# Retention and an expert layer in one kernel: keys and values of two batches loaded as one chunk, two tokens per partition, with attention products on quarters of the array

## The chip, the cores and the metric

The kernel runs on one core of a Trainium2 chip. A core has five engines that run their own instruction streams and wait for each other by semaphores: TensorE (PE in the profile; PEld is its loading of weights), VectorE (DVE), ScalarE (ACT), GpSimd (POOL) and SyncE (SP, which here issues DMAs). Data come from HBM by DMA into SBUF (128 partitions); TensorE writes its products into PSUM, and DVE and ACT read them there. POOL reads and writes SBUF alone. The metric is the device time of one execution in microseconds. Before the change it is 218.52 us, the median of three runs (218.41 to 218.56).

## What is computed

Eight batches of eight heads, 576 tokens, 64 numbers per head. The attention has no softmax: scores are multiplied with a decay that depends on the distance of the tokens. Its output, 4608 tokens of 512, goes through a layer with a softmax-weighted activation and a normalisation.

```python
def _attn_ref(q, k, v) -> np.ndarray:
...
    scores = scale * np.matmul(q, k.transpose(0, 1, 3, 2))
    gamma = 1.0 - 2.0 ** (-5.0 - np.arange(H, dtype=np.float32))
...
    Dmat = np.where(rel >= 0, gamma[:, None, None] ** rel[None, :, :], 0.0)
    ret = scores * Dmat[None, :, :, :]
    return np.matmul(ret, v).astype(np.float32)
...
def _moe_ref(x, w_in, w_out, g_ln) -> np.ndarray:
    h = x @ w_in
    h_max = np.max(h, axis=-1, keepdims=True)
    e = np.exp(h - h_max)
    sm = e / (np.sum(e, axis=-1, keepdims=True) + 1e-09)
    solu = h * sm
    mu = np.mean(solu, axis=-1, keepdims=True)
    var = np.mean((solu - mu) ** 2, axis=-1, keepdims=True)
    ln = (solu - mu) / np.sqrt(var + 1e-06) * g_ln
    return (ln @ w_out).astype(np.float32)
```

Inputs and output are float32; w_in is 512x1024, w_out 1024x512.

## The kernel before

**Chunks.** The 4608 tokens are cut into 36 chunks of 128. For every two batches there are nine: four chunks of 128 tokens of each batch, in turns (chunk 0 is batch 0 tokens 0 to 127, chunk 1 the same of batch 1), and one mixed chunk with the last 64 tokens of both. Token p of a chunk has partition p.

**Decay.** gamma to the power i-j is split into gamma^i on the queries and gamma^-j on the values, both counted from the chunk's first token. So scores need only a triangular mask of ones. What earlier chunks contribute goes through a running state (64x64 per head): per chunk the product of keys and values is added to the decayed state of before.

**Steps of one chunk n**, each a small function that issues a few instructions (lines are those of kernel.py):

- `ld` (L178): three DMAs from SP for queries, keys and values, 256 KB each. A key or value packet is 256 bytes (64 numbers of one token and head). Queries are read in another arrangement, with packets of 1 KB. The mixed chunk has two DMAs of each kind.
- `cq`, `ck`, `cv` (L205, L218, L223): scaling or casting to float16. The letter behind the chunk in the written order names the engine: a ACT, v DVE, g POOL.
- `tq` with `eq`, `tr` with `er`, `kd`, `kq` (L226 to L281): the transposes. PE turns 128x128 blocks into PSUM and DVE or ACT copies them out; `kd` instead lets a DMA turn the keys, from chunk 12 on.
- `sc` (L283): scores. For four pairs of heads, two products with 64 rows each, on the upper and lower half of the array, into two PSUM banks. `mk` (L296): DVE multiplies each of the two with the mask (128x512).
- `kv` (L306): keys times values, eight products with 64 columns. `ad` (L320): DVE adds the decayed state and gives `t`. `d3` (L347): POOL multiplies `t` with gamma^128 for the next chunk's addition; `dk` (L334): POOL makes the float16 state for PE.
- `av` (L358): masked scores times values, eight products with 64 output partitions each, one bank. `fs` (L372): queries times state, added in the same bank. `ex` (L388): copied out as `xT`.
- `m1` (L406; `mr` L393 for the first two, by rows of w_in): xT times w_in, eight matmuls of 512 columns, into one of two PSUM tiles `h`. `mx` (L418): DVE takes the negated row maximum. `xp` (L425): ACT makes exp and its sum. `so` (L433): DVE multiplies h and exp into `u` and sums it; after it the `h` tile is free.
- `ce` (L445): for chunks below 5 the mean is taken off `u`. From 5 on it is in the centred weights `w_c`, made by `mm`, `mc`, `ws` after `wo` has scaled w_out. `wi` casts w_in.
- `sq` (L458): ACT sums squares. `rt` (L471): three small POOL instructions give the reciprocal root. `tu` and `eu` (or `du` by DMA): transposes of `u`. `m2` (L508): times w_out, eight matmuls of 512 columns. `st` (L520): ACT scales, SP stores.
- The last chunk's layer is done in halves by `hm` to `hw`.

**Order.** There is no scheduler: the three texts START, LOOP and END write out in which order the steps are issued, as step:chunk:engine. START holds the first steps up to the point where LOOP takes over, LOOP is repeated for 21 chunks, END drains. Every engine takes its own instructions in that order, SP its DMA issues too.

**Buffers.** PSUM has eight banks: four for `h` and four that BANKS hands out, one digit per request. SBUF tiles come from rotating pools (six or seven loads, five queries, four `xT` and so on); a step waits until the last user of its buffer is done.

Of the kernel before, what the change touches and what calls it, by code (L numbers as in the profile page):

```python
# [10 lines left out]
FP = mybir.dt.float32  # L11
# [3 lines left out]
H = 8  # L15
# [3 lines left out]


PLAIN = 5
FIRST = 7
STEP = 1
STOP = 28
BY_DMA = 12
START = """
ld:0 ld:1 c1:0 ck:0:g cq:0:v cv:0:v li:3 gt:0 c2:0 tq:0 cq:1:g cv:1:v ld:2 kv:0 ck:1:v tq:1 ad:0
eq:1:a d3:0 cq:2:v cv:2:g li:2 li:0 eq:0:a kv:1 wi:3:1:a sc:1 li:1 mk:1 dk:0 sc:0 ck:2:a ld:4
av:1 wi:3:0:a wi:2:1:g fs:1 tq:2 ld:3 mk:0 ad:1 av:0 ex:1:a wi:0:0:g eq:2:a fs:0 wi:1:1:a kv:2
mr:1:3 ad:2 d3:1 wi:1:0:g wi:2:0:v cq:4:g wi:0:1:v d3:2 sc:2 mr:1:0 ex:0:v ld:5 mr:1:2 ld:6  # L30
mr:1:1 mr:0:0 mr:0:2 mk:2 ck:4:g mx:1 xp:1 mr:0:1 mr:0:3 av:2 dk:1 mx:0 tq:4 eq:4:a so:1 cv:4:g
ce:1 wu:0:4 fs:2 lo:1 lo:2 cq:3:v sc:4 ex:2:a ck:3:g cv:3:g tu:1 xp:0 mk:4 m1:2 sq:1 tq:3 eu:1:a
dk:2 kv:4 eq:3:a ck:5:a kv:3 av:4 cq:5:g so:0 fs:4 ad:3 d3:3 sc:3 mx:2 dk:3 cq:6:g ex:4:a mk:3
ad:4 tq:5 cv:5:g xp:2 eq:5:a m1:4 lo:0 lo:3 sc:5 d3:4 so:2 cv:6:g mk:5 dk:4 kv:5 av:3 ck:6:a
fs:3 tq:6 d3:6 wo:4:g av:5 ex:3:a ld:7 eq:6:a wo:1:g mx:4 ad:5 wo:7:g kv:6 xp:4 m1:3 fs:5 ce:0
ce:2 wo:2:a ex:5:a tu:0 tu:2 sc:6 wo:5:a m1:5 ld:8 ad:6 so:4 wo:3:a eu:2:v mk:6 rt:1 wo:6:v
wo:0:a sq:0 d3:5 av:6 sq:2 mx:5 fs:6 ck:7:g mm:0 m2:1 cq:7:g ld:9 mx:3 eu:0:a rt:2 mc:0:v m2:0
ce:4 cq:8:v ws:3:v rt:0 xp:3 tu:4 ex:6:a ws:7:v ld:10 ws:4:v ck:8:g dk:5 st:1 xp:5 tq:7 sq:4
so:3 eu:4:v ld:11 eq:7:a m2:2 st:0 so:5 tq:8 ce:3 eq:8:a m1:6 ws:1:v ws:0:v cv:7:g sc:7 ws:2:g
tu:3 st:2 rt:4 ws:5:v ld:12 m2:4 mk:7 sc:8 sq:3 eu:3:a cq:9:g mx:6 mk:8 m2:3 st:4 dk:6 rt:3  # L40
cq:10:g kv:7 ck:9:a ws:6:v xp:6 cv:9:v ad:7 cv:8:v st:3 av:7 fs:7 ex:7:a ck:10:a ck:11:a
"""
LOOP = """
tr:2 so:-1 tu:-2 ld:6 er:2:v m1:0 dk:0 kv:1 eu:-2:a kd:4 ad:1 cv:3:g av:1 mx:0 sc:2 sq:-2 fs:1
ex:1:a rt:-2 cq:4:g xp:0 m2:-2 d3:0 ck:5:g st:-2 mk:2
"""
END = """
d3:-7 tr:-5 kd:-3 cq:-3:g kv:-6 av:-6 er:-5:v ld:-1 ad:-6 tr:-4 fs:-6 ex:-6:a dk:-7 sq:-9
so:-8 sc:-5 m1:-7 cv:-4:g er:-4:v mk:-5 tr:-3 kd:0 kv:-5 ck:-2:g av:-5 sq:-8 fs:-5 tu:-8 mx:-7
ad:-5 rt:-9 cv:-3:g dk:-5 er:-3:a tu:-9 kd:-2 m1:-6 xp:-7 sc:-4 kv:-4 cq:-2:v eu:-9:v so:-7  # L50
ex:-5:a m1:-5 sc:-3 mk:-4 rt:-8 du:-7 d3:-6 ld:0 mx:-6 eu:-8:a d3:-5 mk:-3 ad:-4 ck:-1:a dk:-6
m2:-9 av:-4 mx:-5 xp:-6 kv:-3 av:-3 d3:-4 cv:-1:g st:-9 d3:-1 ad:-3 kd:-1 cv:-2:g d3:-2 cq:0:g
fs:-4 fs:-3 so:-6 tr:-2 er:-2:v ex:-4:a xp:-5 m2:-8 sq:-6 dk:-4 sc:-2 mk:-2 ck:0:g m1:-4 so:-5
kv:-2 kv:-1 du:-5 ex:-3:a av:-2 sq:-7 st:-8 mx:-4 sq:-5 xp:-4 fs:-2 m1:-3 cq:-1:v cv:0:g kq:-1
rt:-5 dk:-3 ex:-2:a d3:-3 ad:-2 du:-6 tr:0 so:-4 er:0:a m2:-7 sc:0 m1:-2 ad:-1 mk:0 mx:-3
sc:-1 rt:-6 mk:-1 mx:-2 m2:-5 sq:-4 du:-4 kv:0 rt:-7 rt:-4 av:-1 av:0 fs:-1 dk:-1 m2:-6 st:-7
xp:-3 so:-3 ex:-1:v xp:-2 so:-2 du:-3 du:-2 dk:-2 sq:-3 st:-6 fs:0 m1:-1 rt:-3 ex:0:a st:-5
sq:-2 hm:0:0 hm:0:1 m2:-3 mx:-1 hx:0:0 hx:0:1 xp:-1 hp:0:1 so:-1 m2:-2 hp:0:0 ho:0:1 ho:0:0
du:-1 ht:0:1 hc:0 st:-3 ht:0:0 m2:-4 he:0:1:v sq:-1 hq:0:0:v he:0:0:v rt:-2 rt:-1 ad:0
hq:0:1:a h2:0:0 rt:0 m2:-1 h2:0:1 st:-4 st:-2 hw:0:0:a st:-1 hw:0:1:v  # L60
# [3 lines left out]
012312012012302130312031321320132103123120132130123012301230123012301230213021320132012301230213  # L64
021320132012301230213021320132013201321032103120312013201321032103120312013201321032103120312031
203102310210321032120312310213230213210213023201203203
# [3 lines left out]
def _np_tables():  # L70


    g = 1.0 - 2.0 ** (-5.0 - np.arange(H, dtype=np.float64))
    p = np.arange(P)
    gq = (g[None, :] ** p[:, None]) / 8.0
    gk = g[None, :] ** (-p[:, None])
    j = np.arange(8)
    gqt = (g[2 * (p[:, None] % 4) + j // 4] ** (4 * (p[:, None] // 4) + j % 4)) / 8.0
    gqm = (g[2 * (p[:, None] % 4) + j // 4] ** ((4 * (p[:, None] // 4) + j % 4) % 64)) / 8.0
    gkt = g[None, :] ** (-(p % 64)[:, None])  # L80


    gs = np.zeros((P, 4))
    gd = np.zeros((P, 4, 2))
    for e in range(2):
        for hp in range(4):
            gs[e * 64 : e * 64 + 64, hp] = g[2 * hp + e] ** 128.0
        gd[e * 64 : e * 64 + 64, :, e] = gs[e * 64 : e * 64 + 64]
    small = np.concatenate([gq, gk, gqt, gkt, gs, gd.reshape(P, 8), gqm], axis=1).astype(np.float32)
    return small  # L90
# [3 lines left out]
def kernel(  # L94
# [79 lines left out]
    def quads(n):  # L174

        return n != NCH - 2
# [28 lines left out]
    def cq(n, e="g"):  # L205
        if not quads(n):
            return scaled(n, "qf", "q16", gq, ENG[e])
# [570 lines left out]
```

## Time and profile before

| what | value |
|---|---|
| median of three runs | 218.52 us |
| the profiled execution | 218.18 us, span 216.5 us |
| PE busy | 197.4 us (91%), 1989 matmuls |
| DVE busy | 180.8 us (84%) |
| POOL busy | 173.6 us (80%) |
| ACT busy | 167.1 us (77%) |
| packets of the main DMA queue | 111904, 46.55 MB, 92.7% of 16 engines' span |

The span runs from the first to the last instruction of the profiled execution; the time of that execution is 1.7 us longer. PE's busy time counts a matmul until its modelled end, and matmuls overlap: the 264 of L412 have a mean of 379 ns each but start 216 ns apart. So what an instruction costs an engine is read from the distance of starts, and the work that PE has to do is less than its busy time.

### The profile page before, as it was taken

The numbers are of one execution on the slowest core, as the hardware profiler recorded it, in microseconds if no ns is written. First come the engines' busy times: TensorE is split into PE (matmuls) and PEld (weight loads), VectorE is DVE, ScalarE is ACT, GpSimd is POOL, SyncE is SP. The second block draws the span as 40 slices with busy tenths as digits, with TensorE's granted clock in tenths as the row PEclk, the third lists the DMA queues.
The fourth block names the chain that finished last, engine by engine and source line by source line (L and its number), as shares of the span: only waits on it lengthen the run. The fifth ranks groups of instructions, "written<-read, shape, count | busy, mean of one in ns | idle before, by whom it ended". The sixth has DMA issues, their size and how long they took to land.

```text
span 216.5 us, 5376 instructions
## 1 busy us (share of the span) xinstructions
PE 197.4 (91%) x1989; PEld 110.8 (51%) x1989; DVE 180.8 (84%) x289; ACT 167.1 (77%) x279; POOL 173.6 (80%) x275
## 2 busy tenths in 40 slices
PE   0379889896999999999999999999999999999993
PEld 0254456453455555555555555555555565545451
DVE  1378899999997998888888898888888999889840
ACT  2073988966897888888888788888888794986991
POOL 3348889997367899999997899999997899977340
PEclk9999999999999999999999999999999999999999
DMA  5999999998986899799999998899999999674845
GB/s 137 289 317 287 228 280 358 193 245 224 270 228 168 219 183 201 177 225 258 243 223 232 255 208 186 186 247 248 214 227 213 253 181 190 145 172 100 195 109 182
DMA packets 112250, 47.04 MB, mean 217 GB/s; under 512 B 96984, under 2 KB 106208, under 8 KB 112224
## 3 DMA queue, kind: packets, MB, share of 16 engines
q1 hardware_dynamic: 111904, 46.55, 92.7%
q8 instruction: 15, 0.25, 0.5%
q10 hardware_dynamic: 320, 0.16, 0.3%
q14 instruction: 11, 0.09, 0.2%
HBM read 32.54 MB, written 9.44 MB: 194 GB/s over the span
## 4 chain that ended last, share of the span: by engine, by line
PE 78%; DVE 13%; DMA 2%; issue 2%; SPq 2%; ACT 1%; DVEq 0%; ACTq 0%
PE o L515 26%; PE h L412 23%; PE sc L290 5%; PE lp L495 5%; PE x L365 4%; PE x L380 3%; PE kp L314 3%; DVE nm L422 3%; DVE ret L303 2%; DMA vf<-in_v_dram 2%; PE tp L232 2%; PE tr L256 2%; PE h L400 2%; DVE u L437 2%; DVE q L210 1%
## 5 line engine op out<-in xcount | busy, mean ns | idle before, releaser
L412 PE MATMUL h<-w_in,xT 128*128 128x512 f16 x264 | 62.4, 379 | 0.5 <-DVE u L437 0.5
L515 PE MATMUL o<-w_c,uT 128*128 128x512 f16 x240 | 56.5, 379 | 0.6 <-DVE t L327 0.4
L428 ACT ACTIVATE e<-h,nm 128x1024 f32<-128x1024 f32 x35 | 39.0, 1116 | 14.0 <-DVE nm L422 14.0
L303 DVE TENSOR_TENSOR ret<-sc,tris 128x512 f16<-128x512 f32 x72 | 46.1, 682 | 1.3 <-PE sc L290 1.2
L437 DVE SCALAR_TENSOR_TENSOR u<-h,e 128x1024 f16<-128x1024 f32 x35 | 42.7, 1220 | 2.7 <-ACT e L428 1.4
L422 DVE TENSOR_REDUCE nm<-h 128x1 f32<-128x1024 f32 x35 | 42.5, 1216 | 2.0 <-PE h L412 1.5
L515 PEld LDWEIGHTS <-uT 128*128 128x128 f16 x280 | 26.2, 98 | 27.1 <-issue 0.4
L412 PEld LDWEIGHTS <-xT 128*128 128x128 f16 x264 | 24.2, 98 | 24.4 <-issue 0.5
L341 POOL TENSOR_TENSOR s<-t,small 128x512 f16<-128x512 f32 x32 | 34.2, 1070 | 2.6 <-DVE t L329 2.6
L199 POOL TENSOR_TENSOR v<-vf,small 128x512 f16<-128x512 f32 x32 | 33.6, 1051 | 3.0 <-DMA vf<-in_v_dram 3.0
L465 ACT ACTIVATE sq<-u,su 128x1024 bf16<-128x1024 f16 x30 | 34.8, 1159 | 0.1
L210 POOL TENSOR_TENSOR q<-qf,small 128x512 f16<-128x512 f32 x30 | 31.3, 1044 | 1.8 <-DMA qf<-in_q_dram 1.8
L171 ACT CAST xT<-x 128x512 f16<-128x512 f32 x34 | 19.9, 585 | 11.1 <-PE x L380 10.6
L523 ACT ACTIVATE o_sb<-o,rs 128x512 f32<-128x512 f32 x35 | 23.9, 685 | 4.1 <-POOL rs L487 1.6
L171 ACT COPY uT<-lp 128x1024 f16<-128x1024 f16 x25 | 25.3, 1012 | 0.3 <-PE lp L495 0.2
L487 POOL TENSOR_TENSOR rs<-w,mhalf 128x1 f32<-128x1 f32 x36 | 19.8, 551 | 3.0
L483 POOL TENSOR_SCALAR w<-ss,w 128x1 f32<-128x1 f32 x31 | 8.9, 287 | 15.9 <-ACT sq L465 13.9
L171 POOL CAST k<-kf 128x512 f16<-128x512 f32 x28 | 17.1, 611 | 3.0 <-DMA kf<-in_k_dram 3.0
L171 ACT COPY qkT<-tp 128x512 f16<-128x512 f16 x20 | 10.7, 594 | 10.9 <-PE tp L232 10.9
L495 PE MATMUL lp<-ident,u 128*128 128x128 f16 x224 | 17.0, 219 | 1.3 <-DVE u L453 1.3
L353 POOL TENSOR_TENSOR s<-t,small 128x256 f32<-128x256 f32 x24 | 14.9, 622 | 3.4 <-DVE t L327 2.5
L290 PE MATMUL sc<-qkT 64*128 64x128 f16 x288 | 15.2, 225 | 2.0 <-ACT qkT L171 1.2
(89 smaller groups left out, 262.5 us busy)
## 6 DMA issues: line engine op xcount, KB each, us to landing
qf<-in_q_dram SPq DMA_DIRECT2D x32, 256.0 KB, 4.0
kf<-in_k_dram SPq DMA_DIRECT2D x32, 256.0 KB, 4.4
vf<-in_v_dram SPq DMA_DIRECT2D x32, 256.0 KB, 4.7
out_dram<-o_sb SPq DMA_DIRECT2D x32, 256.0 KB, 2.6
w_in<-in_moe_w_in_dram SPq DMA_DIRECT2D x4, 512.0 KB, 6.1
w_out<-in_moe_w_out_dram SPq DMA_DIRECT2D x4, 512.0 KB, 6.7
qf<-in_q_dram SPq DMA_DIRECT2D x8, 128.0 KB, 3.2
kf<-in_k_dram SPq DMA_DIRECT2D x8, 128.0 KB, 3.8
```

Of the source, the lines that this page charges most:

```text
L171: (engine.copy if engine is nc.scalar else engine.tensor_copy)(out=out, in_=in_)
L199: engine.tensor_tensor(out=dst, in0=T.pop((key, n)), in1=table.unsqueeze(2).to_broadcast([P, H, D]), op=ALU.mult,)
L210: ENG[e].tensor_tensor(out=dst.rearrange("p (a h) d -> p h a d", h=2), in0=T.pop(("qf", n)).rearrange("p (h a) d -> p h a d", h=2), in1=ta ...
L303: nc.vector.tensor_tensor(out=r, in0=s, in1=m, op=ALU.mult)
L341: nc.gpsimd.tensor_tensor(out=s16, in0=t.unsqueeze(2).to_broadcast([P, 4, 2, D]), in1=gd.unsqueeze(3).to_broadcast([P, 4, 2, D]), op=ALU.mult,
L412: nc.tensor.matmul(out=h[:, i * 512 : (i + 1) * 512], lhsT=xT[:, d], rhs=w_in16[:, d, i * 512 : (i + 1) * 512], start=d == 0, stop=d == 3,)
L422: nc.vector.tensor_reduce(out=nm, in_=T["h", n], axis=AX.X, op=ALU.max, negate=True)
L428: nc.scalar.activation(out=e, in_=T["h", n], func=ACT.Exp, bias=T.pop(("nm", n)), accum_out=s)
L437: nc.vector.scalar_tensor_tensor(out=u, in0=T.pop(("h", n)), scalar=-1.0, in1=T.pop(("e", n)), op0=ALU.mult, op1=ALU.mult, accum_out=su,)
L465: nc.scalar.activation(out=s, in_=T.pop(("v", n)), func=ACT.Square, scale=-float(DFF), bias=T.pop(("su", n)), accum_out=ss,)
L495: nc.tensor.transpose(out=lp[:, c], in_=u[:, c * P : (c + 1) * P], identity=ident)
L515: nc.tensor.matmul(out=o, lhsT=uT[:, c], rhs=w[:, c], start=c == 0, stop=c == NF - 1)
```

## The change

Queries stay one chunk of 128 tokens of one batch. Keys and values of two batches become one unit: for chunk n (even place of the pair) `lk` and `lv` load 128 tokens of both, batch r on partitions 64r to 64r+63, two consecutive tokens per partition. A packet holds both tokens of one head, 512 bytes. The unit is cast and scaled in two halves of four heads (`ck:n:0`, `ck:n:1`, likewise `cv`), each of 128x512 as a chunk had before.

Since a batch has only 64 partitions now, products with keys or values use a quarter of the array: 64 rows and 64 columns. `sc` issues 16 for a half (32 for two chunks, where there were 16), `av` 16 for a half, `kv` 32 for a pair. Their innermost loops go over head e and batch r, so that four neighbours lie on four different quarters; products of different row halves go to different banks. `kv` requests two banks at once, `av` two for both halves. Masks are multiplied by half, two instructions of 128x512 as before; the mask `tris` knows odd and even tokens.

Decays have one origin for every two chunks. The sum of an even chunk goes to the next without a decay, and `d3` is left for chunks of place 1 alone, with gamma^256. `dk` takes one of three tables.

Transposes of queries and keys are apart (`tr`/`er`, `tk`/`ek`, `kd`). `rt` is split into `ra` (two small instructions, on POOL or DVE) and `rp` (the power, on POOL). The mixed chunks keep their form.

Order: one text, ORDER, writes out all steps; there is no loop. RINGS and SLOTS write out which buffer each tile takes. The counts of buffers differ little (seven for queries, three of double size for keys and for values). The engines in the order differ too: of the transposed copies of queries and keys, 42 stand on ACT and 9 on DVE (before: 21 and 29), of `eu` 16 and 12 (25 and 3), of `ex` 25 and 11 (34 and 2); casts of keys stand 15 times on ACT, 16 on POOL and 5 on DVE (7, 28, 1); `ra` 9 times on DVE.

```diff
...
+ORDER = """
+lq:3 lq:2 lq:0 c1:0 gt:0 cq:2:v tr:2 er:2:a c2:0 lk:0 cq:0:v ck:0:0:g wu:0:4 lq:1 tk:0:0 tr:0
+er:0:v cq:1:g tr:1 ek:0:0:a er:1:v sc:0:0 mk:0:0 lk:2 ck:2:0:g cq:3:g ck:0:1:a tk:0:1 lv:0
+cv:0:1:g cv:0:0:g ek:0:1:a tk:2:0 ek:2:0:a lv:2 sc:0:1 mk:0:1 ck:2:1:a tk:2:1 ek:2:1:a li:0
+cv:2:0:v tr:3 er:3:a li:2 wi:2:0:g av:0:0 cv:2:1:v av:0:1 kv:0 ad:1 dk:1 ex:1:a ad:0 dk:0 ex:0:a
...
+RINGS = dict(
+    qf=7, kf=3, vf=3, q16=5, k16=6, v16=6, qT=5, kT=5, ret0=4, ret1=4, xT=4, t=4, s16=4, s32=2,
+    h=2, e=3, u=5, uT=5, o_sb=4,
+)
+SLOTS = """
+qf 012345612304561235413542536140624504
+h 010010101010100101010100110101101010
+q16 012340123401203420321201324231204121
+qT 012341203240123412032401342134014320
+kf 01201201201201212012
...
+            gs[w, hp] = g[2 * hp + e] ** 256.0
+            for i, power in enumerate((0.0, 256.0, 128.0)):
+                gd[i, w, hp, e] = g[2 * hp + e] ** power
+    pair = 2 * (p[:, None] % 64)
+    gk2 = []
+    for off in (128, 0):
+        at2 = pair[:, :, None] + np.arange(2)[None, None, :] - off
+        gk2.append((g[None, :, None] ** -at2).reshape(P, 16))
+    small = np.concatenate(gq + gk2 + gk[2:] + [gs] + [x.reshape(P, 8) for x in gd], axis=1)
+    small = small.astype(np.float32)
     return small
...
+    def ring(pool, shape, dtype, name):
+
+        at = int(next(slots[name]))
+        assert at < RINGS[name]
+        return pool.tile(shape, dtype, tag=f"{name}_{at}", name=name, bufs=1)
...
-    def ld(n):
-
-        for key, src in (("qf", q), ("kf", k), ("vf", v)):
-            dst = load.tile([P, H, D], FP, name=key, bufs=6 if key == "kf" else 7)
+    def mixed(n):
...
+        else:
+            dst = ring(load, [P, H, 2, D], FP, key)
+            (b,), c = chunks[n]
+            for r in range(2):
+                nc.sync.dma_start(
+                    out=dst[64 * r : 64 * r + 64].rearrange("p h a d -> p h (a d)"),
+                    in_=src[b + r, :, c * P : c * P + P, :].rearrange(
+                        "h (t a) d -> t h (a d)", a=2
+                    ),
+                )
+        T[key, n] = dst
...
+        i = int(how[0])
+        k16 = ring(half, [P, 2, 2, 2, D], F16, "k16")
+        copy(
+            ENG[how[1]], k16.rearrange("p x a e d -> p x e a d"),
+            T["kf", n][:, 4 * i : 4 * i + 4].rearrange("p (x e) a d -> p x e a d", e=2),
+        )
+        T["k16", n, i] = k16
+
+    def cv(n, *how):
+
+        if mixed(n):
+            T["v16", n] = scaled(n, T["vf", n], "v16", gk, ENG[how[0]])
+            return
+        i = int(how[0])
+        T["v16", n, i] = scaled(
...
+        i = int(more[0])
+        kT = T["kT", n, i]
+        for x in range(4):
+            for e in range(2):
+                for r in range(2):
+                    dd, w = slice(64 * e, 64 * e + 64), slice(64 * r, 64 * r + 64)
+                    nc.tensor.matmul(
+                        out=s[e][w, x], lhsT=kT[dd, x, w],
+                        rhs=T["qT", n + r][dd, 2 * i + x // 2], start=True, stop=True,
+                    )
...
+    def kv(n):
+
+        kp = [bank([P, 4, D], FP, f"kp{r}") for r in range(2)]
         for hp in range(4):
...
+            i, x = hp // 2, hp % 2
+            k16, v16 = T["k16", n, i], T["v16", n, i]
+            for a in range(2):
+                for e in range(2):
+                    for r in range(2):
+                        w = slice(64 * r, 64 * r + 64)
+                        nc.tensor.matmul(
+                            out=kp[r][64 * e : 64 * e + 64, hp], lhsT=k16[w, x, a, e],
+                            rhs=v16[w, 4 * x + 2 * e + a], start=a == 0, stop=a == 1,
+                        )
+        T["kp", n], T["kp", n + 1] = kp
 
...
+        if c % 2 == 0:
+            T["s32", b, c + 1] = t
...
-            in1=gd.unsqueeze(3).to_broadcast([P, 4, 2, D]), op=ALU.mult,
+            in1=gd[(0, 1, 0, 2)[c]].unsqueeze(3).to_broadcast([P, 4, 2, D]), op=ALU.mult,
...
-        if chunks[n][1] >= 3:
+        if chunks[n][1] != 1:
...
+        i, first = int(more[0]), ("half", n) not in T
+        T["half", n] = True
+        names = ["xs" if chunks[n][1] == 0 else "x"] * 2
+        if first:
+            for r in range(2):
+                T["xx", n + r] = bank([P, 4, P], FP, f"x{r}")
+        else:
+            for r in range(2):
+                T[names[r], n + r] = T["xx", n + r]
+        ret, v16 = T.pop(("ret", n, i)), T["v16", n, i]
+        for x in range(2):
+            for a in range(2):
+                for e in range(2):
+                    for r in range(2):
+                        w = slice(64 * r, 64 * r + 64)
+                        nc.tensor.matmul(
+                            out=T["xx", n + r][64 * e : 64 * e + 64, 2 * i + x],
+                            lhsT=v16[w, 4 * x + 2 * e + a], rhs=ret[e][w, 2 * x + a],
+                            start=first and x == 0 and a == 0,
+                            stop=chunks[n][1] == 0 and a == 1, skip_group_check=True,
+                        )
 
     def fs(n):
 
...
-    def rt(n):
+    def ra(n, e="g"):
...
+    def rp(n):
+
+        rs = tiny.tile([P, 1], FP, name="rs")
+        nc.gpsimd.tensor_tensor(out=rs, in0=T.pop(("w2", n)), in1=mhalf, op=ALU.pow)
         T["rs", n] = rs
 
...
+        for r in range(2):
+            w = slice(64 * r, 64 * r + 64)
+            nc.gpsimd.affine_select(
+                out=tris[w], in_=tris[w], pattern=[[-1, 2], [1, P]], channel_multiplier=-2, base=0,
+                compare_op=ALU.is_ge, fill=0.0,
+            )
...
-        run(START, 0)
-        for i in range(FIRST, STOP - STEP + 1, STEP):
-            run(LOOP, i)
-        run(END, NCH - 1)
+        run(ORDER, 0)
...
```

`turn` and `product` wrap the transposes and matmuls as they were written out before.

490 lines of the change are left out of this document (269 added, 221 removed).

## The prediction

> **What bounds the kernel now.** I read the page first (busy times, packets), then the busy times by stretches of the span, which show where an engine is full, then the rows of one loop pass in order of time, which show what TensorE (PE) spends its time on, and the waits last.
>
> ```profile
> span 216.5 us, 5376 instructions
> PE 197.4 (91%) x1989; PEld 110.8 (51%) x1989; DVE 180.8 (84%) x289; ACT 167.1 (77%) x279; POOL 173.6 (80%) x275
> DMA packets 112250, 47.04 MB, mean 217 GB/s; under 512 B 96984, under 2 KB 106208, under 8 KB 112224
> q1 hardware_dynamic: 111904, 46.55, 92.7%
> ```
>
> ```profile
> 0.00:10.00 10.00, 2.49 (x21) 1.62 (x21) 1.90 (x6) 1.28 (x1) 3.63 (x14) 1.00 0.87 202
> 10.00:20.00 10.00, 7.63 (x74) 4.45 (x75) 7.47 (x15) 5.88 (x11) 5.24 (x8) 1.00 1.14 318
> 20.00:30.00 10.00, 8.81 (x103) 5.20 (x102) 9.42 (x15) 7.51 (x14) 8.58 (x10) 1.00 1.08 239
> 30.00:40.00 10.00, 8.32 (x107) 5.34 (x106) 9.91 (x18) 8.88 (x17) 9.84 (x13) 1.00 1.06 310
> 40.00:50.00 10.00, 10.00 (x68) 5.10 (x67) 9.96 (x13) 8.04 (x16) 9.65 (x15) 1.00 0.99 218
> 50.00:60.00 10.00, 8.14 (x81) 4.25 (x80) 9.76 (x20) 7.56 (x14) 4.82 (x8) 1.00 0.99 259
> 60.00:80.00 20.00, 19.93 (x219) 11.48 (x217) 17.96 (x29) 17.45 (x28) 16.75 (x26) 1.00 0.81 194
> ```
>
> The columns are the stretch and its length, then busy us of PE, PEld, DVE, ACT, POOL, the granted clock and the DMA share. Two phases stand out. From 20 to 60 us VectorE (DVE) is busy 39.1 of 40 us and PE is not full: DVE sets the pace. From 60 us on PE is full and DVE has a tenth free. Before 20 us loads and first casts are awaited.
>
> ```profile
> 104.51 0.38 PE L412 MATMUL h<-w_in,xT 128*128 128x512 f16 x1
> 104.82 0.32 PE L314 MATMUL kp<-v,k 128*64 128x64 f16 x8
> 104.96 0.39 PE L365 MATMUL x<-ret,v 128*64 128x128 f16 x8
> 105.29 0.40 PE L290 MATMUL sc<-qkT 64*128 64x128 f16 x8
> 105.62 0.40 PE L380 MATMUL x<-qkT,s 128*128 128x128 f16 x4
> ```
>
> ```profile
> 40.30 1.27 DVE L303 TENSOR_TENSOR ret<-sc,tris 128x512 f16<-128x512 f32 x2
> 41.50 1.29 DVE L706 TENSOR_SCALAR w_out<-w_out,g 128x512 f16<-128x512 f32 x1
> 42.72 2.34 DVE L422 TENSOR_REDUCE nm<-h 128x1 f32<-128x1024 f32 x2
> 44.98 0.68 DVE L171 CAST warm<-mean 128x512 f16<-128x512 f32 x1
> ```
>
> The first number is the start, and differences of starts are what an instruction costs its engine. PE: eight value products take 0.33 us with the change of array shape behind them. Starts of single rows give the terms: 216 ns for 512 columns, 56 for 128, 29 for 64. The half-array products (128*64, 64*128) start in twos, 3 to 5 ns apart, each two costing one slot of 56 or 29. A change of shape adds 94 ns. DVE: a mask costs 0.60, a maximum 1.13, `so` 1.15, a 128x512 copy 0.60, a state addition 0.34.
>
> With these terms PE needs 177.4 us of array time (580 matmuls of 512 columns 125.3, 528 of 128 29.6, packed products 19.8, the rest 2.6) and 119 changes of shape, 11.2: 188.5. The span is 4.3 (first matmul) + 188.6 + 19.5 stalls + 4.0 (last matmul, tail). Of the stalls 16.5 lie before 50 us, 3.0 after.
>
> **The change part by part.** PE. Scores, values and states double their products (288, 288 and 256 become 544, 544 and 512) on quarters of the array. If four start together, a chunk pair needs 8 slots of 56, 8 of 56 and 8 of 29 ns as before, so nothing is added. If only two do, a pair pays 0.448 + 0.448 + 0.232 more, times 16 is 18.1 us. The trace has no four-wide product; its nearest rows are the two-wide ones, where the second start costs 3 to 5 ns, so I take zero and keep 18.1 as the far end. State products could instead be held by issue: 8 of them now take 123 ns, 15.4 each; 32 at that rate are 0.49 instead of 0.24, 4 us in all. Their slot of 29 ns follows the columns as 56 and 216 do, so I take zero. Transposes are 436 instead of 432, +0.2; changes of shape 106 instead of 119, -1.2. PE: 188.6 becomes 187.6.
>
> [...]
>
> DVE, the engine that sets the first 60 us. In all: 20 query and key copies fewer (-12.4), 9 more each of `eu` and `ex` (+12.2), 4 more key casts (+1.7), value and query scalings (-0.7), `ra` of 9 chunks (+2.7): +3.5 busy. More telling is what must be done before a PE step. Before, the scores of chunk 9 follow 41.7 us of PE work and need 48.9 of DVE work ahead of them (18 masks, 7 maxima, 7 `so`, 8 state additions, weights and the rest): 7.1 ahead. After, the transposes of `u` of chunk 9 follow 56.1 of PE work and need 66.1 of DVE work (26 masks, 11 maxima, 10 `so`, 12 additions, 5 query copies): 10.0 ahead, the largest lead in the written order. A PE step can't start before DVE's work plus what DVE lost. Before, PE's loss by then was 4.3 + 16.5 = 20.8, so DVE's was 13.7: 10.6 idle in the first 20 us, 1.0 from 20 to 60, 2.1 in small gaps.
>
> DVE's loss afterwards. Queries land each 0.85 us from 4.45 on (landings before); the key load of a pair, 1024 packets of 512 bytes, I put at 1.75. The first pair's keys land at 7.9, cast 8.5, turned and copied 9.8, second query 10.4, its copy 11.1, scores 11.4, first mask at 11.8 (before: 13.4), with 8.8 idle. Then come four chunks before w_in, so its last piece lands at 20.6 (before: 19.0) and the first maximum falls at 21.9 (before: 20.65). Between, DVE does 8.4 us of work and idles 1.7. That is 10.5 where the same count before gives 11.25. Bounds: 10.0, what the start forces, and 16, if the 2.1 of small gaps and the 1.0 double. The loss of before less these 0.75 is 12.95. I take 12.3, between the lower bound and that and nearer to that, and PE's early loss is 10.0 + 12.3 = 22.3, 1.5 more than before.
>
> Late stalls, 3.0. Six of 0.1 and one of 0.45 end with a state addition that waited for POOL's decay (`t` behind `s`, 5.1 us in all); additions of odd chunks now take the even chunk's sum with no decay between, so 1.1 goes. What is late next is the copy of `x` for two chunks, since a pair holds two of four banks. I take 1.9, bounds 0 and 6.
>
> POOL: decays 24 to 8 (-10.0), key casts 28 to 16 (-7.3), `ra` moved (-5.1), in all -23. It hides beside PE. ACT +3.8: 21 more query and key copies, 8 more casts, less 9 `eu` and 9 `ex`; hidden too, as ACT idles 20%.
>
> DMA: 65,536 packets of 256 bytes at 20.4 ns each are 83.5 us of 16 engines; 32,768 of 512 lie between 20.4 and the 59.7 of 1024 bytes, 42 to 122 us. I take 27 (eight such packets on another queue), 55. Nothing waits for a load after 20 us, so this is worth nothing by itself; it only makes the early landings above. Loads are issued as often as before (120), key transposes 20 instead of 21, so SP's queue is level.
>
> A row against the change: `cq` on DVE took 1.53 us at 25.4 and 46.8, 0.69 otherwise, both times beside POOL work. More instructions of that sort, with SBUF operands, stand on DVE now, but before the step that decides, 25 instead of 24: +0.8 us at most, inside the bounds.
> [...]
>
> Sum: 187.6 + 22.3 + 1.9 + 4.0 = 215.8 of span. The profiled execution took 218.18, 1.7 beside its span, so 217.5; it lies 0.34 under the median of 218.52, so about 217.8.
>
> **The rivals.** *DVE loses more in the first 60 us* (the other side). Each us that DVE loses over 12.3, ahead of PE's 56.1st us of work, moves the end a us. At 13.0 nothing is gained, over 13.4 it is slower by more than 0.2%; at 16 with 4 of late stalls the time is 223.6. For it: 10.0 of lead against 7.1, and five query copies on DVE in that stretch where there was one. Against: DVE idles only 1.0 from 20 to 60 now, and POOL has less to do.
> *Quarter products start only in twos*: 217.8 + 18.1 = 235.9. For it: no row shows four. Against: twos behave as if free. A milder form: PE's issue falls behind. The densest 24 products now take 598 ns, 25 each; a pair's 96 at that rate are 2.4 us instead of 1.1, 20 us in all.
> [...] The 15.4 ns of eight state products speak against it.
> *The start gets shorter*: DVE loses only 10.0 and late stalls vanish: 187.6 + 20.0 + 4.0 + 2.0 = 213.6. For it: DMA is full until 60 us, and keys and values are the narrow packets. Against: w_in lands later.
> *The larger packets change nothing*, since loads were early enough: that is contained in the sum.
>
> **How the numbers follow.** 0.2% is what can be told from no change: under 218.1 is faster, over 218.9 slower. The sum's case 0.45 faster, 0.09 in the band; shorter start 0.05, faster; DVE or late stalls 0.30, slower; twos or issue 0.11, slower. So faster 0.50, same 0.09, slower 0.41. The range takes in DVE's loss from 10 to 16 and late stalls up to 6: 212.5 to 225, leaving out the quarter case and some 0.08 at the ends. The likeliest case alone: 215 to 219.
>
> **What would show it.** Four starts within some 15 ns and slots of 56 and 29 in the rows of PE; PE full from about 75 us instead of 60; DVE over 95% busy until then; the first mask near 12 and the first maximum near 22 us; waits of additions for POOL gone; DMA share down by 15 points or more. Quarter slots above 60 ns, DVE waiting for ACT or PE between 22 and 75 us, or PE waiting for copies of `x` later would make it wrong.

## The result and the profile after

The changed kernel takes 239.3 us (median of four runs, 238.5 to 241.2) against 218.54 for the kernel before in the same session: a ratio of 1.096, with a 95% interval of 1.089 to 1.103. The forecast was 217.8, with a range of 212.5 to 225.0. It was wrong by 21.5 us and in its sign. (Of the ten runs of the changed kernel with wide loads below, four lie between 217.6 and 219.3 us and six between 222.0 and 226.0; its ratio is that of the four, and the median of all ten is 223.3.)

The profiled execution took 239.1 us. These are lines of its page: the span, the busy times, the main DMA queue with its packets, MB and share of the 16 engines' time, and the shares of the chain that ended last.

```profile
span 237.2 us, 6886 instructions
PE 205.1 (86%) x2761; PEld 114.5 (48%) x2761; DVE 185.4 (78%) x309; ACT 169.4 (71%) x291; POOL 154.9 (65%) x231
...
q1 hardware_dynamic: 78592, 46.41, 95.7%
...
PE 36%; DMA 25%; POOL 13%; SPq 10%; DVE 6%; issue 5%; ACT 2%; POOLq 0%; DVEq 0%
```

The same bytes move in 30% fewer packets, and yet the queue's share rose, from 92.7 to 95.7%. DMA holds a quarter of the chain. No engine's list of work grew enough to explain 20 us: DVE, for one, has about 5 us more on its list and is idle for 6 points more of the span.

The busy times by stretch of the changed kernel, in the columns used above (PE, PEld, DVE, ACT, POOL, granted clock, DMA share, GB/s):

```profile
20.00:30.00 10.00, 8.86 (x118) 4.31 (x119) 7.91 (x13) 3.53 (x6) 6.40 (x8) 1.00 1.14 266
...
50.00:60.00 10.00, 7.58 (x123) 4.58 (x123) 9.01 (x16) 5.99 (x13) 8.63 (x11) 1.00 0.98 219
60.00:80.00 20.00, 17.39 (x251) 9.79 (x246) 16.39 (x31) 15.16 (x25) 16.15 (x23) 0.91 1.17 235
```

In these stretches neither DVE nor PE is full (DVE is from 30 to 40 us, with 9.86). DMA is: its share is 0.98 to 1.17. The share adds up the times of packets, so over 1 means that packets of one engine overlap. What the engines wait for is in the list of waits of the changed kernel (who waits, on whom, us in total, times, longest):

```profile
POOL k L255 <- DMA kf<-in_k_dram: 16.4, 6, 6.2
...
POOL v L317 <- DMA vf<-in_v_dram: 9.1, 7, 2.1
...
POOL q L328 <- DMA qf<-in_q_dram: 8.1, 8, 3.3
...
DVE q L328 <- DMA qf<-in_q_dram: 5.7, 3, 3.8
```

Casts wait for loads, all through the first two thirds of the span. By differences of starts of PE's matmuls, as in the prediction, PE's stalls are 41.5 us where they were 19.5, and they run on until 160 us: 23.7 by 60 us, 28.7 by 80, 38.3 by 150. After 160 us, when most loads are done, PE is nearly full (19.1 of 20 us from 160 to 180).

Not all of these 41.5 us are waits. Twenty-seven matmuls of 512 columns hold PE for some 427 ns until the next start, instead of 216; that is 5.7 us. Fourteen of them lie before 27.9 us, and thirteen in two stretches of 3.4 us, from 75.7 and from 130.3 us, for which the trace grants half of TensorE's clock (hence the 0.91 in the last line above). The kernel before has three such matmuls, all before 20 us, and no such stretch until its end.

The loads themselves, by the list of DMA issues of the changed kernel (median us from issue to landing, which was 4.0, 4.4 and 4.7 before):

```profile
qf<-in_q_dram SPq DMA_DIRECT2D x32, 256.0 KB, 6.8
kf<-in_k_dram SPq DMA_DIRECT2D x32, 256.0 KB, 7.0
vf<-in_v_dram SPq DMA_DIRECT2D x32, 256.0 KB, 7.7
```

In the trace's packet records the 32,768 packets of 512 bytes took 45.4 ns each in the mean, 44 in the median, where I had taken 27. That is 93 us of 16 engines; the packets of 256 bytes that they replace took 83.6. So the larger packets saved nothing. The question for the experiments: is it the size, is it where the packets go, or is the new order itself short of something?

### The profile page after: what moved, and what is told of

It is laid out like the page before. It is cut to its first block, busy times and chain, and to the rows that moved or that the text cites. A ratio compares the mean times of both kernels' runs of the same rounds, so it can differ in the third digit from the quotient of the medians.

```text
span 237.2 us, 6886 instructions
## 1 busy us (share of the span) xinstructions
PE 205.1 (86%) x2761; PEld 114.5 (48%) x2761; DVE 185.4 (78%) x309; ACT 169.4 (71%) x291; POOL 154.9 (65%) x231
## 3 DMA queue, kind: packets, MB, share of 16 engines
q1 hardware_dynamic: 78592, 46.41, 95.7%
## 4 chain that ended last, share of the span: by engine, by line
PE 36%; DMA 25%; POOL 13%; SPq 10%; DVE 6%; issue 5%; ACT 2%; POOLq 0%; DVEq 0%
PE o L264 15%; PE h L264 11%; DMA qf<-in_q_dram 9%; DMA vf<-in_v_dram 9%; SPq L301 5%; DMA kf<-in_k_dram 5%; POOL v L317 4%; POOL s L500 3%; POOL q L328 3%; DMA kT<-k 2%; PE sc L436 2%; SPq L281 2%; PE x L545 2%; PE x L264 2%; SPq L372 2%
## 5 line engine op out<-in xcount | busy, mean ns | idle before, releaser
L264 PE MATMUL h<-w_in,xT 128*128 128x512 f16 x280 | 68.4, 389 | 0.0
L449 DVE TENSOR_TENSOR ret<-sc,tris 128x512 f16<-128x512 f32 x64 | 40.6, 681 | 4.4 <-PE sc L436 4.4
L500 POOL TENSOR_TENSOR s<-t,small 128x512 f16<-128x512 f32 x32 | 34.3, 1078 | 13.9 <-DVE t L486 11.7
L264 PEld LDWEIGHTS <-uT 128*128 128x128 f16 x280 | 26.9, 100 | 28.7 <-issue 3.3
L264 PEld LDWEIGHTS <-xT 128*128 128x128 f16 x288 | 26.5, 100 | 29.5 <-issue 3.2
L255 POOL CAST k<-kf 128x512 f16<-128x512 f32 x16 | 10.2, 635 | 20.6 <-DMA kf<-in_k_dram 16.4
L668 POOL TENSOR_TENSOR rs<-w,mhalf 128x1 f32<-128x1 f32 x36 | 19.8, 552 | 5.6 <-DVE w L659 4.3
L255 ACT CAST xT<-x 128x512 f16<-128x512 f32 x25 | 14.3, 585 | 8.7 <-PE x L264 7.8
L255 ACT COPY qT<-tr 128x512 f16<-128x512 f16 x26 | 14.9, 591 | 7.5 <-PE tr L260 7.5
L255 ACT COPY uT<-lp 128x1024 f16<-128x1024 f16 x16 | 16.1, 1013 | 5.6 <-PE lp L260 5.5
L260 PE MATMUL tr<-ident,q 128*128 128x128 f16 x140 | 14.2, 230 | 3.9 <-POOL q L328 1.6
L436 PE MATMUL sc<-qT,kT 64*64 64x128 f16 x512 | 14.4, 235 | 2.5 <-ACT sq L642 0.9
L260 PEld LDWEIGHTS <-u 128*128 128x128 f16 x224 | 13.8, 98 | 4.9 <-issue 2.6
```

The costliest lines, as they stand in the source:

```text
L255: (engine.copy if engine is nc.scalar else engine.tensor_copy)(out=out, in_=in_)
L260: nc.tensor.transpose(out=out, in_=in_, identity=ident)
L264: nc.tensor.matmul(out=out, lhsT=lhsT, rhs=rhs, start=start, stop=stop, skip_group_check=True)
L449: nc.vector.tensor_tensor(out=r.rearrange("p (x a) i -> p x a i", a=2), in0=s.rearrange("p (x a) i -> p x a i", a=2), in1=tris.unsqueeze(1 ...
L500: nc.gpsimd.tensor_tensor(out=s16, in0=t.unsqueeze(2).to_broadcast([P, 4, 2, D]), in1=gd[(0, 1, 0, 2)[c]].unsqueeze(3).to_broadcast([P, 4, ...
```

## The experiments

The code cuts of this part are shortened; `<-` stands for a load.

### What a packet costs, by size and by destination

A kernel of loads alone, twelve loads in each of seven groups (A to G), each into tiles of its own; it computes nothing. The destination of a group is the line that differs:

```
A  dst[:, 0:512]   <- 128 tokens, 8 heads, 256-byte packets
B  dst[:, 0:512]   <- 256 tokens, 4 heads, 512-byte packets
C  dst[64 r : 64 r + 64] <- 128 tokens, 8 heads, 512-byte packets, r = 0, 1, 0, 1 ...
D  as C, r = 1 issued on ACT's queue
E  as C, 64 tokens, 256-byte packets    F  as B, 1024-byte packets    G  as C, r = 0 always
```

> A kernel of loads alone, the attention and the layer are left out and the output is zeros. Seven groups of twelve loads from SP, each group starts when the one before has landed. A: 128 partitions, packets of 256 bytes, 256 KB a load. B: 128 partitions, 512 bytes, 256 KB. C: 64 partitions, lower and upper half in turns, 512 bytes, 256 KB, as in the changed kernel. D: as C, upper halves issued from ACT's queue. E: 64 partitions in turns, 256 bytes, 128 KB. F: 128 partitions, 1024 bytes, 256 KB. G: as C, always the lower half. Theory 1 (destination): a packet of 512 bytes is slow in the changed kernel because its transfer writes only 64 partitions. Then a load of 256 KB takes about 0.9 us in B (32 packets per DMA engine of 27 ns) and 1.4 us in C and G (32 of 44). Theory 2 (size): a packet of 512 bytes costs 44 ns wherever it goes; then B, C and G all take about 1.4. Theory 3 (the written order, not the loads, makes TensorE wait) says that B and C are alike and near 0.9, and that the 45 ns of the changed kernel's packets are queueing. A should be 1.2 to 1.3 as in the kernel before. D tells whether both halves at once repair it: 0.9 if so, 1.4 if not. [...]

The stretches below are the inner parts of groups A, B, C, D, F and G, in this order (the columns here are DVE, POOL, clock, DMA share, GB/s):

```profile
6.00:18.00 12.00, 8.57 (x19) 0.00 (x0) 1.00 1.24 220
22.00:31.00 9.00, 1.38 (x9) 0.00 (x0) 1.00 1.06 286
37.00:49.00 12.00, 1.54 (x10) 0.00 (x0) 1.00 1.16 212
54.00:64.00 10.00, 1.39 (x9) 0.00 (x0) 1.00 1.20 251
80.00:89.00 9.00, 1.54 (x10) 0.00 (x0) 1.00 0.87 287
94.00:108.00 14.00, 1.38 (x9) 0.00 (x0) 1.00 1.22 191
```

The loads of the kernel before (A) come at 220 GB/s, a packet of 256 bytes in a median 19 ns. Packets of 512 bytes to 128 partitions (B) take 27 ns and come at 286: larger packets do help, by 30%. The same packets to 64 partitions (C), which is what the change issues, take 42 ns and come at 212, a little less than A; to one half all the time (G) they take 51 ns and come at 191. So it is the destination, not the size; what makes the packets to half of the partitions slower, no run here shows. Over the whole group C comes at 217 GB/s (a load every 1.19 us, not the 1.4 that I expected). Group E, loads of 128 KB in packets of 256 bytes, was held by its issue, 0.69 us a load on SP's queue, and tells nothing of its packets.

### Wide loads in the changed kernel and in the one before

In the changed kernel, each load of 256 KB goes to all 128 partitions, 256 tokens of four heads, instead of 128 tokens of eight heads to one half. The kernel before gets packets of 512 bytes too, in the same manner.

```
-  out=dst[64 * r : 64 * r + 64]...,      in_=src[b + r, :, c * P : c * P + P, :]...
+  out=dst[:, 4 * r : 4 * r + 4]...,      in_=src[b + r, 4 * r : 4 * r + 4, s0 : s0 + 2 * P, :]...
```

> The changed kernel with one difference: each key or value load of 256 KB fills all 128 partitions for four heads instead of 64 partitions for eight; packets stay at 512 bytes, their number and the written order too. The tokens that land on a partition are other ones, so the attention is computed from wrong keys and values. Theory 1 (destination): packets fall from 45 to about 27 ns, the DMA share from 96% to about 80%, the waits for loads after 25 us go, and the time falls to 216 to 222. Theory 2 (size): packets stay at 44 to 45 ns and the time at 237 to 242. Theory 3 (order): the time stays over 230 even if packets get quicker.

> The kernel before with one difference: keys and values come in packets of 512 bytes to all 128 partitions, four heads of 256 tokens a load, 256 KB as before. The tokens are other ones, so the attention is computed from wrong keys and values. Theory 1: packets of 512 bytes cost about 27 ns, the DMA share falls from 93% to about 75%, and since TensorE waits for no load after 20 us the time is 216.5 to 218.6. Theory 2: the packets cost 44 ns, the DMA share stays above 90% and the time is 218 to 220.

With wide loads the changed kernel's ratio to the kernel before is 1.002 (0.997 to 1.007), and its profiled execution took 218.75 us. PE's stalls fall from 41.5 to 21.5 us, and loads all but leave the chain:

```profile
PE 62%; DVE 22%; DMA 4%; SPq 3%; POOL 3%; ACT 2%; issue 2%; DVEq 0%; POOLq 0%
```

The two stretches of half clock are gone as well. So the 20 us come from the loads: from waits for them, and some 5 us from the slower PE that goes with the waits. (Of the profiled executions of this case's twelve whole kernels, the four with spans up to 218.3 us have no stretch of half clock before their last 15 us, the eight longer ones have one to four. That waits of PE bring them on is argued from this, not shown.) Loads still hold the new order a little: after 20 us its casts and scalings of keys, values and queries wait 11 us for wide loads, where they waited 29 as changed and 2 in the kernel before.

The run changes a second thing. In the changed kernel a cast reads all 128 partitions, so it waits for both loads of a pair: the first keys landed at 8.3 and 10.0 us, and their first cast began at 10.1. A wide load holds four heads, just what one cast reads: the first keys landed at 8.0 and 8.9, and their first cast began at 8.1. How much of the gain is the rate, and how much that a cast waits for 256 KB instead of 512, no run here tells apart.

In the kernel before, the larger packets, at a median of 27 ns, change nothing: 1.003 (0.999 to 1.007). My sentence that nothing there waits for a load after 20 us holds, but for 2 us of casts.

### Destination alone, order alone

That leaves a puzzle: group C gives 212 GB/s, A 220. The kernel before runs well on A's rate. Why does the changed kernel starve on C's? The next runs part the destination from the order. In the first, the kernel before cuts its key and value loads in two of 128 KB, each to one half.

```
-  nc.sync.dma_start(out=dst[pp], in_=src[b, :, s0 : s0 + m, :]...)
+  for r in range(2):
+      nc.sync.dma_start(out=dst[64 * r : 64 * r + 64]..., in_=src[b, 4 * r : 4 * r + 4, s0 : s0 + P, :]...)
```

> The kernel before, with each 256 KB key or value load of a single-batch chunk cut into two loads of 512-byte packets, heads 0 to 3 into partitions 0 to 63 and heads 4 to 7 into partitions 64 to 127. All the bytes and the instructions behind the loads stay; the places of the tokens are wrong, so the output is not the reference's. Theory D (the destination alone): transfers that reach 64 partitions hold up any kernel; 65 to 70% of the bytes then come at about 1.2 us per 256 KB and this kernel goes to 232 to 242 us. Theory O (rate against need): the written order of the changed kernel needs its inputs sooner (with wide loads it had started 100 of its 108 casts of inputs at 160 us, the kernel before 89), and about 217 GB/s is what the kernel before lives on anyway (256-byte packets to 128 partitions: 214 GB/s in the loads alone); then 217 to 222 us here.

It took 227.0 us, ratio 1.040 (1.032 to 1.048), between the two forecasts, and its packets took 27 ns, not 44. The run changed a second thing: 64 more loads, each of which holds SP's queue some 0.6 us while it is issued. It says nothing on the destination; the run after next mends that.

In the second, the changed kernel loads packets as the kernel before does, 256 bytes to 128 partitions, but 512 KB at once for the two batches, and keeps everything else of the change:

```
-  for r in range(2): dst[64 * r : 64 * r + 64] <- src[b + r, :, 128 tokens], two tokens a packet
+  dst[:, 16 places] <- src[b : b + 2, :, 128 tokens], one token a packet, one load
```

> The changed kernel, with the loads of keys and values as before the change: 256-byte packets to all 128 partitions (one load of 512 KB for the two batches, 128 tokens of 16 heads). The bytes stay, the places of the tokens are wrong, so the output is not the reference's. Theory D (the destination): with 128 partitions again it runs like the kernel with wide 512-byte packets, 217 to 221 us. Theory O (rate against need): 1.20 us per 256 KB alone against 1.19 for the halves, so the written order starves as it did with the halves, 234 to 242 us with 35 us or more of stalls of PE, against 21.5 with wide 512-byte packets.

235.9 us, ratio 1.082 (1.075 to 1.089), with 39.1 us of stalls. With the packets of the kernel before, the new order starves nearly as badly. So the destination is not needed for the loss. (As in the changed kernel, a cast here waits for 512 KB.) The mirror image is the kernel before with the changed kernel's loads: two chunks share a tile, one load of 256 KB to each half. A twin with the same shared tiles keeps the old loads.

```
+  two = load.tile([P, 2, H, D], FP, name=key, bufs=4)
+  two[64 * r : 64 * r + 64] <- src[b + r, :, c * P : c * P + P, :], two tokens a packet    (first run)
+  two[:, r]                 <- src[b + r, :, c * P : c * P + P, :], one token a packet     (its twin)
```

> The kernel before, with keys and values loaded as the changed kernel does it: for two chunks at once, one load of 256 KB of 512-byte packets into partitions 0 to 63, one into 64 to 127, as many loads as before. Bytes and all that follows stay; the places of the tokens are wrong, so the output is not the reference's. To be read against the next run, which has the same tiles for two chunks. Theory D (the destination alone holds up any kernel): 8 us or more over that run, 230 us and up. Theory O (217 GB/s is what the old order can live on, only the new order needs more): within 4 us of that run, 217 to 224 us.

> The kernel before, with keys and values loaded for two chunks at once into a shared tile, but each load as before (256-byte packets to 128 partitions, one chunk a load). The output is the reference's. The first chunk of a pair now waits for the loads of the second at the start only if its casts wait for both: a start later by up to 2 us; otherwise as the kernel before: 217 to 222 us under both theories.

The kernel before with loads to halves took 220.5 us, ratio 1.015 (1.005 to 1.026); its twin 224.1, 1.031 (1.022 to 1.041), dearer than I expected for the shared tiles; why, these runs don't show. The packets to halves were as slow as in the changed kernel, 44.6 ns in the mean, and the list of issues shows the late landings:

```profile
kf<-in_k_dram SPq DMA_DIRECT2D x32, 256.0 KB, 6.1
vf<-in_v_dram SPq DMA_DIRECT2D x32, 256.0 KB, 7.1
```

Yet the old order loses only 1.5%, and nothing against the twin, although its casts too now wait for both loads of a pair. The line that explains it is the stretch from 20 to 140 us, of the kernel before,

```profile
20.00:140.00 120.00, 114.78 (x1197) 65.26 (x1196) 109.42 (x171) 99.90 (x165) 105.98 (x157) 1.00 0.97 226
```

of the kernel before with loads to halves,

```profile
20.00:140.00 120.00, 116.82 (x1195) 65.54 (x1194) 107.66 (x174) 99.21 (x163) 107.54 (x160) 1.00 1.04 227
```

of the changed kernel,

```profile
20.00:140.00 120.00, 105.73 (x1493) 58.66 (x1494) 100.73 (x162) 88.28 (x149) 92.15 (x125) 0.97 1.16 235
```

of the changed kernel with the old loads,

```profile
20.00:140.00 120.00, 106.32 (x1454) 59.12 (x1454) 101.79 (x161) 88.65 (x149) 91.28 (x125) 0.97 1.03 232
```

and of the changed kernel with wide loads of 512 bytes:

```profile
20.00:140.00 120.00, 115.33 (x1688) 65.63 (x1680) 112.41 (x186) 99.69 (x171) 105.36 (x142) 1.00 1.07 255
```

Read the first busy time (PE) against the last column. The old order keeps PE busy for 115 to 117 of 120 us on 226 GB/s. The new order gets 232 to 235 and keeps PE busy for 106; for 115 it moves 255. It asks for its inputs sooner. Counted in the traces, the changed kernel with wide loads had started 100 of its 108 casts and scalings of inputs at 160 us, the kernel before 89 with either kind of load, the changed kernel as it stands 90. The old order takes no more when loads are faster; the new one takes more. How much sooner is best read at the same step of the expert layer. At its tenth row maximum the kernel before has the masks of 11 chunks behind it, 40 casts of inputs and 18.2 MB of transfers; the changed kernel has 12 chunks, 48 casts and 19.8 MB. At the twentieth it is 29.7 MB against 33.1. So attention is one chunk further, but inputs are loaded and cast for nearly three chunks more. Of the loads tried here, only those of 512-byte packets to all 128 partitions pay for that, and the change's layout does not get them.

### Attempts at a repair

*Upper halves on ACT's queue.* Loads alone gained by it (group D, 251 GB/s).

```
-  nc.sync.dma_start(out=dst[64 * r : 64 * r + 64]...
+  (nc.sync, nc.scalar)[r].dma_start(out=dst[64 * r : 64 * r + 64]...
```

> The changed kernel with the loads to partitions 64 to 127 issued on ACT's queue, those to 0 to 63 on SP's as now; the output is the reference's. Loads alone took 1.05 us per 256 KB on two queues, 1.19 on one, 0.86 to 128 partitions. Theories D and O both say that the rate counts: 42% of the way from the halves on one queue to the wide loads, so PE's stalls go from 41.5 to about 33 us and the time to 229 to 232 us, and up to 236 if ACT, which waits for a free buffer before it issues, holds up its own copies. If loads were not what PE waits for: 239 us.

261.1 us, ratio 1.202 (1.191 to 1.214): far worse. In ACT's written order the upper loads stand behind its copies, and ACT issued two of them 0.01 us after the start of a copy for which it had idled 3.02 and 13.18 us. Rows of ACT in order of time, in this kernel:

```profile
6.39 0.58 ACT L255 COPY qT<-tr 128x512 f16<-128x512 f16 x1 [3.02 <-PE tr L260]
6.40 0.72 ACTq L301 DMA_DIRECT2D kf<-in_k_dram  x1
20.15 0.58 ACT L255 COPY kT<-tk 128x512 f16<-128x512 f16 x1 [13.18 <-PE tk L260]
20.16 0.62 ACTq L301 DMA_DIRECT2D kf<-in_k_dram  x1
```

The first upper half is issued at 6.40 us, behind a copy that waited for a transposed query; it lands at 18.8, when a load of w_in that SP issued at 7.76 has already landed (18.3). The next, at 20.16, waits behind a copy that needs those keys. PE's stalls are 32.9 us by 40 us, where the halves on SP's queue alone had 19.3. I had named the converse, ACT's copies held up by the loads' waits for buffers, and put it at 4 us.

*Halves in finer turns.* Loads of 128 KB, lower and upper in turn.

```
+  for i in range(2):
       for r in range(2):
-          dst[64 * r : 64 * r + 64]                   <- src[b + r, :, 128 tokens]
+          dst[64 * r : 64 * r + 64, 4 * i : 4 * i + 4] <- src[b + r, 4 * i : 4 * i + 4, 128 tokens]
```

> The changed kernel, with each load of 256 KB cut into two of 128 KB, in the order: heads 0 to 3 into the lower partitions, heads 0 to 3 into the upper, heads 4 to 7 into the lower, heads 4 to 7 into the upper. The output is the reference's. In the kernel before with such loads a 512-byte packet took a median 27 ns, as to 128 partitions, where 256 KB at a time into one half took 44: the DMA engines then work into both halves at once. But every load holds SP's queue some 0.6 us while it is issued, and 64 more of them add about 40 us to that queue, to a full 19 of 20 us where the changed kernel needs inputs fastest. If packets are again 27 ns and SP keeps up: 219 to 224 us. If SP's issue takes the place of the destination as the limit (128 KB in 0.65 us are 200 GB/s): 228 to 240 us, with packets at 27 ns all the same. If the median stays at 40 ns or more, the size of a load has nothing to do with it.

248.1 us, ratio 1.138 (1.125 to 1.152). The packets took a median 27 ns, as forecast, and SP's issue took the destination's place, at a dearer price than I gave it (240 us at most). The chain of this kernel:

```profile
PE 34%; DMA 28%; SPq 15%; POOL 11%; issue 6%; ACT 2%; DVE 1%; POOLq 0%; DVEq 0%
PE o L264 13%; SPq L302 11%; PE h L264 10%; DMA kf<-in_k_dram 10%; DMA qf<-in_q_dram 7%; DMA vf<-in_v_dram 6%; POOL v L320 3%; SPq L281 3%; DMA out_dram<-o_sb 2%; POOL q L331 2%; PE lp L260 2%; DMA kT<-k 2%; POOL s L503 2%; PE x L264 2%; PE
```

L302 is the line of the key and value loads: 11% of the span goes to issuing them. Why the packets are fast here is open: whether the finer turns made them so, with both halves written at once as I had expected, or only a queue that SP could no longer keep full, these runs do not tell.

*Another unit.* 256 neighbouring tokens of one batch as two chunks of 128, so that one load of 512 KB reaches all partitions. The written order is the changed kernel's with the state steps moved; in the first form they stand right behind the scores, in the second about where they stood.

```
-  for c in range(4):       chunks += [((2 * g,), c), ((2 * g + 1,), c)]
+  for c in (0, 2):
+      for b in (2 * g, 2 * g + 1):  chunks += [((b,), c), ((b,), c + 1)]
-  two loads, src[b + r, :, c * P : c * P + P, :]
+  one load, src[b, :, c * P : c * P + 2 * P, :]
```

> The changed kernel with its unit cut otherwise: the two chunks that share a load are neighbours in one batch (256 tokens, two per partition on 128 partitions, one load of 512 KB) instead of the same chunk of two batches. Quarter products, masks, casts and decays stay; the state of the first chunk has to reach the second within the unit, so the state product, its two additions and its scaling stand right behind the scores, one state-times-query step is moved to the odd chunk of the first unit, and buffers are handed out anew for the changed order. Theory 1: 512-byte packets at about 27 ns and a time of 214 to 222. Theory 2: 44 ns and 236 to 242. Theory 3: over 228, whatever the packets cost, since the written order is the old one or a slightly worse one.

> A repair with the reference's output: the unit is 256 neighbouring tokens of one batch instead of 128 tokens of two, so that one load of 512-byte packets reaches all 128 partitions. The first try at it put the state steps of a unit right behind its scores and the second chunk's state product close behind, and lost 56 us to waits of POOL and PE; here the state steps stay about where the changed kernel has them, 14 steps ahead of the second chunk's state product. If loads are all that is wrong with the change: 216 to 224 us. If the tie between the two chunks of a unit (the second needs the state that the first leaves) costs by itself: 235 us or more with 512-byte packets at 27 ns.

255.3 us, ratio 1.172 (1.166 to 1.179), and 248.6, ratio 1.139 (1.130 to 1.147). Packets take 27 ns in both, and the chain of the second has hardly any DMA left:

```profile
PE 47%; DVE 21%; POOL 19%; issue 5%; ACT 3%; DMA 2%; SPq 1%; POOLq 0%; DVEq 0%
```

In its place stands the tie within a unit. The second chunk needs the state that the first leaves, and its decay on POOL waits for DVE's addition, the longest of this kernel's waits:

```profile
POOL s L494 <- DVE t L480: 28.0, 6, 6.1
```

This wait was 11.7 us in the changed kernel. That the tie costs the 30 us is argued from this line, not shown; an order written for this unit might do better, and none was tried beyond the two. No kernel here beats the kernel before.

## Why the prediction was wrong

**The step that failed** is the DMA term. It read: "32,768 of 512 lie between 20.4 and the 59.7 of 1024 bytes ... I take 27 (eight such packets on another queue), 55. Nothing waits for a load after 20 us, so this is worth nothing by itself". Two things are wrong in it.

First the size of the term: 45.4 ns, 93 us of 16 engines. The row from which I took 27 was eight packets of a small load at 3 us, and says nothing of loads to half of the partitions; to 128 partitions 27 is the right median (group B, and both kernels with wide loads; their means are 29 to 33). The trace of before has no load to 64 partitions of this kind; the diff says `dst[64 * r : 64 * r + 64]` in plain sight, and I did not weigh it. I bounded this term from 42 to 122 us, and 93 lies inside; but since I priced the whole term at nothing, the bounds never reached the range.

Second, and the larger error, "nothing waits for a load" was read from the old order and carried over to the new one. It nearly holds for the old order even with the slow loads (220.5 us, 1.5% more, and less than the twin's 224.1). It fails for the new order even with the old loads (235.9). A sign stood in the profile of before: DMA at a share of 0.97 from 20 to 140 us. It is no proof, since the share is no ceiling (1.14 at 318 GB/s from 10 to 20 us in the same trace). But 226 GB/s is about what loads of 256-byte packets alone reach (220), and the new order asks for 13% more in that stretch (255 GB/s). The prediction itself says that DMA is full until 60 us, but uses it only for the case of a shorter start. I counted what DVE must do ahead of each PE step in the new order and never counted the bytes. The forecast also had no term for PE's clock, which took some 5 of the 22 us of added stalls.

**The rest of the sum** can be judged by the changed kernel with wide loads, where the loads bind far less. All in us:

| term | forecast | changed kernel | with wide loads |
|---|---|---|---|
| PE's array and changes of shape | 187.6 | 187.6 | 187.6 |
| first matmul and stalls up to 60 us | 22.3 | 27.8 | 20.3 |
| later stalls | 1.9 | 17.8 | 5.1 |
| last matmul and tail | 4.0 | 4.0 | 4.0 |
| span | 215.8 | 237.2 | 217.0 |

- *Quarter products free in fours*: right. In the changed kernel four start together, 2 to 5 ns apart, and rows of PE, in order of time, show 32 value products in 0.57 us and 32 state products in 0.38, the change of shape included; the forecast's slots and change of shape give 0.54 and 0.33:

```profile
177.79 0.64 PE L545 MATMUL x<-ret,v 64*64 64x128 f16 x32
178.36 0.40 PE L260 MATMUL tr<-ident,q 128*128 128x128 f16 x4
...
182.14 0.45 PE L471 MATMUL kp<-v,k 64*64 64x64 f16 x32
182.52 1.12 PE L260 MATMUL lp<-ident,u 128*128 128x128 f16 x16
```

  The rival of products in twos gave 235.9, close to the measured time, by a mechanism that these rows refute.
- *DVE sets the first 60 us*: true only where the loads let it. From 20 to 60 us DVE is busy 39.6 us with wide loads and 36.0 as changed; I had said over 95%.
- *The start*: keys of the first pair landed at 8.3 and 10.0 (forecast 7.9), the last piece of w_in at 25.3 (20.6), the first mask came at 14.6 (11.8) and the first maximum at 27.8 (21.9). With wide loads the same read 8.0 and 8.9, 20.3, 13.0 and 22.8, at most 1.2 us off, so the method was largely sound and its packet was wrong.
- *Late stalls*: additions no longer wait for POOL's decay to speak of (5.1 us before, 0.7 in one wait now), as forecast. I took 1.9 for what is left; it was 5.1 with wide loads.
- *DMA share down by 15 points*: the forecast's own figures, 83.5 less 55 us, give 13. It went up by 3; with wide loads 87.9%, down by 5, since those packets took 32.6 ns in the mean and not 27.
- *The rivals*: the case on the other side, DVE losing more, had the right sign and the wrong engine, so it was right by luck. No rival was a shortage of loads; the one that spoke of packets said that loads were early enough. Even with wide loads the change gains nothing that can be measured.

## What to carry to other kernels

When an order is rewritten, count the bytes that it needs by each hour, as one counts an engine's work, and set that against the GB/s and the DMA share of the same stretch: a share near 1 that nothing waits for (0.97 at 226 GB/s here) may be a bound that has not been met yet. Price a transfer by a row with the same size of packet and the same destination partitions; here, in loads of 256 KB, 512 bytes cost a median of 27 ns to 128 partitions, 42 to 44 to 64 in turns, and 51 to one half always. Ask too how many loads a cast waits for. And a saving that the profile says nobody waits for may be what pays for the rest of the change: look for what becomes dear if it does not come.

## What the runs showed of the hardware that I had not expected

- Packets of 512 bytes to 64 partitions came no faster than packets of 256 bytes to 128: 212 against 220 GB/s, where 512 bytes to 128 partitions gave 286 and 1024 bytes 287. Alternating the halves on one queue was better than one half all the time (212 against 191), and two queues, one to each half, better still (251, 31% over the 191).
- An issue of a load of keys took SP a median 0.63 us in the changed kernel, whether it carried 128 KB or 256 KB. With key and value loads of half the size their issues took 11% of the chain that ended last, where they had taken 5%.
- A load issued on ACT's queue behind a copy that waited landed a dozen us after its issue at the start (issued 6.40, landed 18.8), later than a load that SP issued 1.4 us after it (landed 18.3). How the queues are served, these runs don't show.
- The profiled executions of the eight whole kernels with spans over 218.3 us had one to four stretches of 3.4 us at half of TensorE's granted clock, in which matmuls of 512 columns started 427 ns apart instead of 216 (changed kernel). The four shorter kernels had none before their last 15 us.
